# Scratch arrays of the last layer's weights laid out by chunks of 128 columns

## The chip, the core and the metric

One core of a Trainium2 chip runs the whole program. The metric is the device time of one execution in microseconds (us), taken as the median of several runs. The engines are PE (matrix products, TensorE), DVE (VectorE), ACT (ScalarE), POOL (GpSimd) and SP, which here only issues transfers. All transfers go through one queue, SP's, in program order.

## The reference

Windowed attention over 4 batches, 8 heads, 576 positions and head size 64 gives x with 2304 rows of 512 columns. Two feed-forward layers follow; the change is in what serves the second one's output product:

```python
gate = 1.0 / (1.0 + np.exp(-(x @ w_gate)))          # 512 -> 1536
x = gate * (x @ w_val) @ w_out                       # 1536 -> 512
h = x @ w_in                                         # 512 -> 2048
g = np.maximum(h, 0.0) + alpha * np.minimum(h, 0.0)
out = g @ moe2_w_out                                 # 2048 -> 512
```

## The kernel before, in words

Every large product is done in float16 with each factor split into a high and a low half, so three matmuls stand for one (high by high, high by low, low by high). The second layer's two products use a seven-product scheme over 2x2 blocks: seven combinations of the weight's blocks times seven combinations of the data's blocks. So the weight `moe2_w_out` (2048 by 512, called `w_out2`) is turned into seven float16 arrays of 1024 by 256, each as high and low half. That is done beside the matmuls of the first layer, in these steps:

- `out2_load`, `out2_decode`, `out2_bound`, `out2_store` (L763 to L784): for each chunk `c` of 128 columns (4) and each half `h` of the rows (2), the weight is read, decoded to float32 by DVE, and stored to the scratch array `plain_dram`.
- `out2_sum` and `out2_power` (L786, L790) make one scale for all of it, from the largest sums.
- For four pieces `(q, c)`, called here the first to the fourth: `out2_fetch` (L796) reads the four blocks of the piece back into two `quarter` tiles; `out2_sums` (L804) makes four combinations on POOL (L810 to L813); `out2_high` (L816) makes the high halves on ACT (L820); `out2_low` (L822) the low halves on DVE (L825); `out2_put` (L834) stores them to the scratch array `w2_dram` (L838). The seven products of a piece lie in four `halves` tiles: products 1 and 2, 3 and 5, 6 and 7, and 4 alone, called tiles A, B, C and D below.
- `w2_fetch` (L1189) later reads one whole product into SBUF, and `out2_mm` (L1195) uses it as the moving operand, 256 columns at a time (L1210).

The `quarter`, `halves`, `words`, `y` and `ys` tiles share one pool of eight buffers (`yp`). A new tile waits until what last used its buffer is done: a store that reads it, or an engine that does. ACT, DVE, POOL and SP each work strictly in program order, so one that waits holds back all that stands behind it. The program counts transfers on eight counters used in turn, so a transfer also waits until the one eight places ahead of it has landed.

The order is written out by hand: a queue of `steps`, each with a cost, is worked off by `prepare` between groups of matmuls. In the last batch (`late`), the output product of the first layer (`o1_mm`, L632) runs through four column groups d = 0 to 3 of 72 matmuls each. `last_output` puts the start of the second layer between them: `y_load` at the start of d = 0 and d = 1, `y_sums` (POOL, L901), `y_high` (ACT, L924) and `y_low` (DVE, L928) in d = 1, and the first matmuls of the second layer (`in2_mm`, L967) after the first 6 matmuls of d = 2. These need `yh`, which ACT and DVE make behind all of `out2_high` and `out2_low`.

Of the kernel before, what the change touches and what calls it, by code (L numbers as in the profile page):

```python
# [8 lines left out]
F32 = mybir.dt.float32  # L9
F16 = mybir.dt.float16  # L10
# [14 lines left out]
def attention_moe_kernel(  # L25
# [22 lines left out]
    nc = tc.nc  # L48
    P = 128
# [4 lines left out]
    NT, DM = out.shape  # L54
    F1 = w_out.shape[0]
    F2 = w_out2.shape[0]
    KD = DM // P
    M1 = F1 // P
    M2 = F2 // P
    U = M2 // 2  # L60
    H4 = DM // 2
# [8 lines left out]
    wp = ctx.enter_context(tc.tile_pool(name="wp", bufs=1))  # L70
# [3 lines left out]
    dp = ctx.enter_context(tc.tile_pool(name="dp", bufs=1, space=bass.MemoryType.DRAM))  # L74
# [410 lines left out]
    plain = {}  # L485
    wt = {}

    def stage():
        return wp.tile([P, 8, P], F32, tag="st", name="plain", bufs=2)

    def flat(t):

        return t.rearrange("p k f -> p (k f)")
# [187 lines left out]
    yh = {}  # L681
    w2p = None
    wi_dram = dp.tile([U, P, 2, 7, 2 * P], F16, name="wi_dram")
    plain_dram = dp.tile([P, M2, DM], F32, name="plain_dram")
    w2_dram = dp.tile([7, P, 2, U, H4], F16, name="w2_dram")

# [91 lines left out]

    def out2_store(c, h):
        nc.sync.dma_start(
            out=plain_dram[:, 8 * h:8 * h + 8, P * c:P * c + P], in_=plain.pop(("2", c, h))
        )  # L784

    def out2_sum():  # L786
# [9 lines left out]
    def out2_fetch(q, c):  # L796

        for h in range(2):
            t = quarter[h] = yp.tile([P, 2, 4, P], F32, tag="y", name="quarter")
            for i in range(2):  # L800
                f = H4 * i + P * c
                nc.sync.dma_start(out=t[:, i], in_=plain_dram[:, 8 * h + 4 * q:8 * h + 4 * q + 4, f:f + P])

    def out2_sums(q, c):  # L804

# [16 lines left out]
    def out2_low(q, c, which):  # L822
        for i in which:
            t = plain["h", q, c, i]
            nc.vector.scalar_tensor_tensor(  # L825
                out=t[:, 1], in0=plain["q", q, c][i], scalar=s_2, in1=t[:, 0], op0=ALU.mult, op1=ALU.subtract
            )
        for a in last_put:
            out2_put(*a)
        last_put[:] = [(q, c, which)]  # L830
# [3 lines left out]
    def out2_put(q, c, which):  # L834
        for i in which:
            t = plain.pop(("h", q, c, i))
            for z in range(2):
                nc.sync.dma_start(  # L838
                    out=w2_dram[i - 1, :, z, 4 * q:4 * q + 4, P * c:P * c + P],
                    in_=t[:, z].rearrange("p (k f) -> p k f", k=4),  # L840
                )

    def alpha_scale():

# [334 lines left out]
    ring = deque()  # L1179
    sums2 = {}  # L1180

    def w2_ring(first):
        if first:
            ring.append([flat(stage()).bitcast(F16).rearrange("p (k f) -> p k f", f=H4) for _ in range(2)])
        else:
            t = wp.tile([P, 3, 2, U, H4], F16, name="w_2", tag="w_o")
            ring.extend([t[:, i, z] for z in range(2)] for i in range(3))

    def w2_fetch(i):  # L1189
# [5 lines left out]
    def out2_mm(j, i, k):  # L1195
        n = blocks[j][1] // 2
        nt = n // P
        first = {1: True, 6: True, 5: True}.get(i, False)
        bank = "xyz"[{1: 0, 2: 0, 6: 1, 7: 1, 4: 1, 5: 2, 3: 2}[i]]
        if first and k == 0:  # L1200
            turn["o"] = (turn.get("o", -1) + 1) % 4
            sums2[bank] = banks[:, turn["o"], :]
        ps, w, g = sums2[bank], w2q[i][0], g2[j, i, k // 2]
        h = g[0][:, :, n * (k % 2):n * (k % 2) + n]
        for t in range(nt):
            c = slice(P * t, P * t + P)
            for z, (a, x_) in enumerate(
                ((h[:, 0, c], w[0][:, k, :]), (h[:, 0, c], w[1][:, k, :]), (h[:, 1, c], w[0][:, k, :]))
            ):
                nc.tensor.matmul(  # L1210
                    ps[:, H4 * t:H4 * t + H4], lhsT=a, rhs=x_, start=(first and k == 0 and t == 0 and z == 0),
                    stop=(k == U - 1 and z == 2), skip_group_check=True,
                )
        g[1] -= 1
        if not g[1]:
            h, _, home = g2.pop((j, i, k // 2))
            if home:
                home[1] -= 1
                h = home[0]
            if not home or not home[1]:  # L1220
                places2.append(h)
        if k == U - 1:
            ring.append(w2q[i].popleft())
            out2_done(j, i, ps[:, :H4 * nt], nt)

    def out2_done(j, i, ps, nt):
        n = H4 * nt
        s_ = total[:, j:j + 1]
        e, u2, u3 = (temps[x_][:, :n] for x_ in ("e", "u2", "u3"))
        dst = {1: e, 6: u2, 2: u3, 7: u3, 5: u3, 4: e, 3: u2}[i]  # L1230
        to = {2: (0, 0), 5: (1, 1), 4: (1, 0), 3: (0, 1)}.get(i)
        if i in (1, 2):
            nc.scalar.activation(dst, ps, AF.Copy, scale=s_)
        else:
            nc.vector.scalar_tensor_tensor(
                out=dst, in0=ps, scalar=s_, in1={6: e, 7: e, 5: u3, 4: e, 3: u2}[i], op0=ALU.mult, op1=ALU.add
            )
        if to:
            r0 = blocks[j][0] + P * nt * to[0]
            nc.sync.dma_start(  # L1240
                out=out[r0:r0 + P * nt, H4 * to[1]:H4 * to[1] + H4].rearrange("(t p) c -> p t c", p=P),
                in_=dst.rearrange("p (t c) -> p t c", c=H4),
            )
# [64 lines left out]
    with tc.manual_schedule():  # L1308
# [66 lines left out]
        for n in range(2 * KD):  # L1375
            c, h = n // 2, n % 2
            step(4, lambda c=c, h=h: out2_decode(c, h, 0))
            step(
                4, lambda c=c, h=h: out2_decode(c, h, 1),
                lambda n=n: out2_load((n + 1) // 2, (n + 1) % 2) if n + 1 < 2 * KD else None,  # L1380
                lambda n=n: out2_store((n - 1) // 2, (n - 1) % 2) if n else in2_store(U - 1),
            )
            step(0, lambda c=c, h=h: out2_bound(c, h), apart=1)
        order = [dict(q=q, c=c) for c in range(2) for q in range(2)]
        step(3, lambda: out2_store(KD - 1, 1), lambda: out2_fetch(**order[0]))
        step(1, out2_sum, out2_power, sums=True, apart=3)
        for n, a in enumerate(order):
            step(0, lambda a=a: out2_sums(**a), lambda n=n: out2_fetch(**order[n + 1]) if n < 3 else None)
            step(0, lambda a=a: out2_high(**a, which=(1, 2)))
            step(3, lambda a=a: out2_high(**a, which=(3, 5)), lambda a=a: out2_low(**a, which=(1, 2)))  # L1390
            step(3, lambda a=a: out2_high(**a, which=(6, 7)), lambda a=a: out2_low(**a, which=(3, 5)))
            step(3, lambda a=a: out2_high(**a, which=(4,)), lambda a=a: out2_low(**a, which=(6, 7)))
            step(2, lambda a=a: out2_low(**a, which=(4,)))
# [117 lines left out]
        i = 2 * turn["m"]  # L1511
# [169 lines left out]
```

## Time and profile before

| what | value |
|---|---|
| runs | 909.71, 910.52, 911.55 us; median 910.52 |
| profiled execution | 908.63 us; its span in the profile 906.8 us |
| mean granted clock of PE | 0.971 of full |
| PE, DVE, ACT, POOL busy | 843.8, 677.8, 450.8, 303.4 us |
| transfers | 166.81 MB in 120439 packets, mean 184 GB/s |

PE is busy 93% of the span, so the question is where its idle time lies and what ends it. In the profile's row of 40 slices, the 24th (521 to 544 us) is the one after the start-up in which PE's busy share falls, to 7 tenths, and its granted clock to 6 tenths; the transfer engines are at 9 tenths there.

### The profile page before, as it was taken

Reading aid. Unit: us, or ns where it says so; the run is one execution under the profiler, and the core shown is the slowest. Engines: PE = TensorE matmul, PEld = TensorE weight load, DVE = VectorE, ACT = ScalarE, POOL = GpSimd, SP = SyncE. Lnnn points to the kernel's source line nnn. Section 1 sums busy time; section 2 is a strip of 40 time slices with the busy share of each in tenths; the row PEclk is TensorE's granted clock in tenths of the full one; section 3 lists DMA queues with packets and bytes.
Section 4 is the critical chain, followed back from the end, with each engine's and each line's share of the span. In section 5 each row is a group of like instructions: output and inputs, shape, how many; then the busy total and the mean of one; then the engine's idle time right before and its main releaser. Section 6 shows DMA issues by size and latency. Waiting matters only on the chain.

```text
span 906.8 us, 19500 instructions
## 1 busy us (share of the span) xinstructions
PE 843.8 (93%) x8196; PEld 696.4 (77%) x8196; DVE 677.8 (75%) x1039; ACT 450.8 (50%) x739; POOL 303.4 (33%) x264
## 2 busy tenths in 40 slices
PE   7778778899999999999999959997999999999998
PEld 5566566687777877778788738886788888888887
DVE  6999999726978757767795647678888878886751
ACT  5676555444444445534435356555456456545430
POOL 2455656500202001111125643335344454243220
PEclk9899899799999999999999969998999999999999
DMA  9763435115215615009758995955765695575462
GB/s 325 263 227 129 146 117 170 40 46 178 81 51 180 199 49 200 25 2 306 247 157 224 242 256 195 338 218 184 267 263 187 214 343 187 197 258 208 143 215 85
DMA packets 120439, 166.81 MB, mean 184 GB/s; under 512 B 34464, under 2 KB 96032, under 8 KB 120352
## 3 DMA queue, kind: packets, MB, share of 16 engines
q1 hardware_dynamic: 120352, 165.58, 54.4%
q8 instruction: 64, 1.05, 0.5%
q14 instruction: 23, 0.19, 0.1%
HBM read 137.24 MB, written 28.31 MB: 183 GB/s over the span
## 4 chain that ended last, share of the span: by engine, by line
PE 59%; DVE 24%; ACT 6%; DMA 5%; issue 3%; SPq 2%; POOL 0%; ACTq 0%; POOLq 0%; DVEq 0%
PE banks L590 16%; PE banks L1210 14%; PE banks L967 13%; PE banks L632 12%; DVE plain L183 4%; DVE plain L187 3%; DVE plain L179 2%; PE banks L437 2%; DMA w_dram<-halves 2%; DVE temp_w L1013 2%; DVE temp_y L1013 1%; DVE gf L608 1%; DVE g_gv L1052 1%; PE banks L323 1%; DMA words<-w_gate 1%
## 5 line engine op out<-in xcount | busy, mean ns | idle before, releaser
L590 PE MATMUL banks<-xh,w_gv 128*128 128x288 f16 x2304 | 294.6, 289 | 1.5 <-ACT sg L603 1.5
L590 PEld LDWEIGHTS <-w_gv 128*128 128x128 f16 x2304 | 224.8, 99 | 60.8 <-issue 1.8
L967 PE MATMUL banks<-yh,w_i 128*128 128x256 f16 x1536 | 191.2, 276 | 19.2 <-ACT yh L924 9.9
L967 PEld LDWEIGHTS <-w_i 128*128 128x128 f16 x1536 | 151.6, 99 | 40.7 <-issue 20.4
L632 PE MATMUL banks<-gt,w_o 128*128 128x288 f16 x1152 | 148.8, 290 | 1.6 <-POOL gt L168 1.5
L632 PEld LDWEIGHTS <-w_o 128*128 128x128 f16 x1152 | 113.0, 99 | 32.2 <-issue 1.8
L1210 PEld LDWEIGHTS <-g_gv 128*128 128x128 f16 x780 | 76.6, 98 | 9.2
L1210 PE MATMUL banks<-w,g_gv 128*128 128x256 f16 x612 | 75.5, 273 | 0.0
L164 POOL TENSOR_SCALAR sc<-sc 128x1 f32<-128x1 f32 x35 | 12.5, 357 | 178.8 <-DVE sc L160 178.7
L1062 POOL TENSOR_TENSOR yh<-temp_y 128x512 f32<-128x512 f32 x16 | 27.1, 1692 | 131.5 <-DVE temp_y L1013 126.8
L194 ACT ACTIVATE junk<-plain 128x1024 bf16<-128x1024 f32 (+1 forms) x36 | 36.3, 1009 | 59.5 <-DVE plain L198 30.1
L187 DVE SCALAR_TENSOR_TENSOR plain<-words,plain 128x512 uint32<-128x512 uint32 x68 | 63.8, 959 | 1.2
L1013 DVE SCALAR_TENSOR_TENSOR temp_w<-neg,sc,temp_w 128x256 f32<-128x256 f32 x48 | 55.5, 1194 | 10.9 <-ACT neg L1005 10.8
L1210 PEld LDWEIGHTS <-g_g 128*128 128x128 f16 x564 | 55.2, 98 | 6.4
L183 DVE SCALAR_TENSOR_TENSOR plain<-words,plain 128x512 uint32<-128x512 uint32 x68 | 58.8, 885 | 1.2
L168 POOL TENSOR_TENSOR gt<-gf,gt 128x576 f16<-128x576 f32 x24 | 36.9, 1538 | 66.4 <-ACT gt L615 66.4
L608 DVE SCALAR_TENSOR_TENSOR gf<-banks,sg 128x576 f32<-128x576 f32 x48 | 36.0, 749 | 30.6 <-PE banks L590 30.1
L603 ACT ACTIVATE sg<-banks,sc 128x576 f32<-128x576 f32 x48 | 35.2, 734 | 34.3 <-PE banks L590 25.2
L615 ACT ACTIVATE gt<-gf 128x576 f16<-128x576 f32 x48 | 32.3, 676 | 39.0 <-DVE gf L608 39.0
L1210 PE MATMUL banks<-w,g_g 128*128 128x256 f16 x396 | 48.3, 273 | 0.0
L179 DVE TENSOR_SCALAR plain<-words 128x512 uint32<-128x512 uint32 x68 | 40.2, 611 | 7.8 <-DMA plain_dram<-plain 3.9
L388 POOL TENSOR_TENSOR s<-s,rs 128x1152 f32<-128x1152 f32 (+1 forms) x9 | 17.8, 1977 | 71.4 <-DVE rs L383 64.1
(170 smaller groups left out, 1284.1 us busy)
## 6 DMA issues: line engine op xcount, KB each, us to landing
w_i<-wi_dram SPq DMA_DIRECT2D x40, 896.0 KB, 6.3
w<-w_dram SPq DMA_DIRECT2D x52, 512.0 KB, 8.5
words<-w_out SPq DMA_DIRECT2D x28, 512.0 KB, 5.4
plain<-w_dram SPq DMA_DIRECT2D x18, 512.0 KB, 8.5
words<-w_in SPq DMA_DIRECT2D x16, 512.0 KB, 5.1
w_dram<-halves SPq DMA_DIRECT2D x56, 128.0 KB, 2.6
q<-qbd SPq DMA_DIRECT2D x6, 1152.0 KB, 6.5
words<-w_gate SPq DMA_DIRECT2D x12, 512.0 KB, 5.1
```

What stands on the lines that cost most here:

```text
L168: engine.tensor_tensor(out=lo, in0=src, in1=hi, op=ALU.subtract)
L179: nc.vector.tensor_scalar(out=d, in0=hi, scalar1=3, scalar2=0x3FFFFFFF, op0=ALU.logical_shift_left, op1=ALU.bitwise_and)
L183: nc.vector.scalar_tensor_tensor(out=d, in0=hi, scalar=0xC0000000, in1=d, op0=ALU.bitwise_and, op1=ALU.bitwise_or)
L187: nc.vector.scalar_tensor_tensor(out=d, in0=lo, scalar=29, in1=d, op0=ALU.logical_shift_right, op1=ALU.bitwise_or)
L194: nc.scalar.activation(junk[:, :src.shape[1]], src, AF.Square, accum_out=dst)
L590: nc.tensor.matmul(ps[:, h, :], lhsT=a, rhs=x_[:, H2 * h:H2 * h + H2], start=(kk == 0 and i == 0), stop=(kk == KD - 1 and i == 2),)
L603: nc.scalar.activation(halves(sg), ps, AF.Sigmoid, scale=sgx[b][:, m:m + 1])
L608: nc.vector.scalar_tensor_tensor(out=halves(gf), in0=ps, scalar=2.0 ** -15, in1=halves(sg), op0=ALU.mult, op1=ALU.mult)
L632: nc.tensor.matmul(ps[:, h, :], lhsT=a, rhs=x_[:, H2 * h:H2 * h + H2], start=(m == 0 and z == 0), stop=(m == M1 - 1 and z == 2),)
L967: nc.tensor.matmul(o, lhsT=h, rhs=l, start=(new and v == 0 and q == 1), stop=(q == total_), skip_group_check=True,)
L1013: nc.vector.scalar_tensor_tensor(out=temps[x_][:, c], in0=t[:, c], scalar=slope[:, u + v:u + v + 1], in1=src[:, c], op0=ALU.mult, op1=ALU.add,
L1210: nc.tensor.matmul(ps[:, H4 * t:H4 * t + H4], lhsT=a, rhs=x_, start=(first and k == 0 and t == 0 and z == 0), stop=(k == U - 1 and z == 2) ...
```

## The change

The two scratch arrays get another layout, so that what one transfer moves for one partition lies in a row in DRAM. A store of `plain_dram` moves 4 KB in a row for each partition (before, 8 rows of 512 bytes), a load of a quarter 2 KB (before, 4 rows of 512 bytes), a store of `w2_dram` 1 KB for each half (before, 4 rows of 256 bytes), with both halves in one transfer. A load of a whole product from `w2_dram` stays at 4 KB in a row. In SBUF its columns now lie as two chunks, so the matmul's moving operand is two rows of 128 columns, 2 KB apart, where it was one row of 256.

```diff
-    plain_dram = dp.tile([P, M2, DM], F32, name="plain_dram")
-    w2_dram = dp.tile([7, P, 2, U, H4], F16, name="w2_dram")
+    plain_dram = dp.tile([P, KD, M2, P], F32, name="plain_dram")
+    w2_dram = dp.tile([7, P, 2, 2, U, P], F16, name="w2_dram")
     def out2_store(c, h):
-            out=plain_dram[:, 8 * h:8 * h + 8, P * c:P * c + P], in_=plain.pop(("2", c, h))
+            out=plain_dram[:, c, 8 * h:8 * h + 8], in_=plain.pop(("2", c, h))
     def out2_fetch(q, c):
-                f = H4 * i + P * c
-                nc.sync.dma_start(out=t[:, i], in_=plain_dram[:, 8 * h + 4 * q:8 * h + 4 * q + 4, f:f + P])
+                nc.sync.dma_start(out=t[:, i], in_=plain_dram[:, 2 * i + c, 8 * h + 4 * q:8 * h + 4 * q + 4])
     def out2_put(q, c, which):
-            for z in range(2):
-                nc.sync.dma_start(
-                    out=w2_dram[i - 1, :, z, 4 * q:4 * q + 4, P * c:P * c + P],
-                    in_=t[:, z].rearrange("p (k f) -> p k f", k=4),
-                )
+            nc.sync.dma_start(
+                out=w2_dram[i - 1][:, :, c, 4 * q:4 * q + 4].rearrange("p z k f -> p z (k f)"), in_=t
+            )
     def w2_ring(first):
-            ring.append([flat(stage()).bitcast(F16).rearrange("p (k f) -> p k f", f=H4) for _ in range(2)])
+            ring.append([flat(stage()).bitcast(F16).rearrange("p (c k f) -> p c k f", c=2, k=U) for _ in range(2)])
-            t = wp.tile([P, 3, 2, U, H4], F16, name="w_2", tag="w_o")
+            t = wp.tile([P, 3, 2, 2, U, P], F16, name="w_2", tag="w_o")
     def out2_mm(j, i, k):
-                ((h[:, 0, c], w[0][:, k, :]), (h[:, 0, c], w[1][:, k, :]), (h[:, 1, c], w[0][:, k, :]))
+                ((h[:, 0, c], w[0][:, :, k, :]), (h[:, 0, c], w[1][:, :, k, :]), (h[:, 1, c], w[0][:, :, k, :]))
-                    ps[:, H4 * t:H4 * t + H4], lhsT=a, rhs=x_, ...
+                    ps[:, H4 * t:H4 * t + H4].rearrange("p (c f) -> p c f", c=2), lhsT=a, rhs=x_, ...
```

The order on PE, ACT, DVE and POOL stays; only line numbers behind L834 fall by 2 or 3. On SP, the rows from the fetch of the fourth piece to the last store, before:

```order
L802 DMA quarter<-plain_dram 128x4x128 x4
L838 DMA w_dram<-halves 128x4x128 x2
L757 DMA w_i_5829<-wi_dram 128x3584
L869 DMA y<-y_dram 128x2x256 x2
L838 DMA w_dram<-halves 128x4x128 x18
L652 DMA y_dram<-y 128x576
L869 DMA y<-y_dram 128x2x512 x2
L838 DMA w_dram<-halves 128x4x128 x10
```

The same rows of the changed kernel:

```order
L801 DMA quarter<-plain_dram 128x512 x4
L836 DMA w_dram<-halves 256x1x512
L757 DMA w_i_5829<-wi_dram 128x3584
L866 DMA y<-y_dram 128x2x256 x2
L836 DMA w_dram<-halves 256x1x512 x9
L652 DMA y_dram<-y 128x576
L866 DMA y<-y_dram 128x2x512 x2
L836 DMA w_dram<-halves 256x1x512 x5
```

The stores are half as many (28 where there were 56 in all), and nothing has changed places.

On ACT, what the high halves of the third and the fourth piece wait for, before. `DMAHW0` to `DMAHW7` are the eight counters of transfers; four of them together are the four stores of the tile that had the buffer before, two of them the two stores of a tile D.

```order
L820 ACTIVATE halves_6257<-quarter_6096,sc_78 128x512 [waits DMAHW2_49,DMAHW7_49,DMAHW1_49,DMAHW0_49]
L820 ACTIVATE halves_6286<-quarter_6099,sc_78 128x512 [waits DMAHW5_49,DMAHW4_49,DMAHW6_49,DMAHW3_49,Activation_49]
L820 ACTIVATE halves_6314<-plain_6245,sc_78 128x512 [waits DMAHW0_49,DMAHW7_49,Activation_49,Pool_49]
L820 ACTIVATE halves_6323<-plain_6246,sc_78 128x512 [waits DVE_49,Pool_49]
L820 ACTIVATE halves_6366<-quarter_6251,sc_78 128x512 [waits DMAHW6_49,DMAHW5_49,DMAHW7_49,DMAHW4_49,DMAHW3_49]
L820 ACTIVATE halves_6369<-quarter_6254,sc_78 128x512 [waits DMAHW2_49,DMAHW3_49,DMAHW1_49,DMAHW0_49]
L820 ACTIVATE halves_6400<-plain_6360,sc_78 128x512 [waits DVE_49,Pool_49]
L820 ACTIVATE halves_6448<-plain_6361,sc_78 128x512 [waits DMAHW1_49,DMAHW0_49]
```

And of the changed kernel, for the same eight instructions (tiles A, B, C and D of the third piece, then of the fourth):

```order
L819 ACTIVATE halves_6244<-quarter_6090,sc_78 128x512 [waits DMAHW2_49,DVE_49]
L819 ACTIVATE halves_6273<-quarter_6093,sc_78 128x512 [waits DMAHW5_49,DMAHW3_49,DMAHW2_49]
L819 ACTIVATE halves_6300<-plain_6232,sc_78 128x512 [waits DVE_49,Pool_49]
L819 ACTIVATE halves_6307<-plain_6233,sc_78 128x512 [waits DVE_49]
L819 ACTIVATE halves_6346<-quarter_6238,sc_78 128x512 [waits DMAHW7_49,DMAHW6_49]
L819 ACTIVATE halves_6349<-quarter_6241,sc_78 128x512 [waits DMAHW1_49,DMAHW0_49]
L819 ACTIVATE halves_6379<-plain_6340,sc_78 128x512 [waits DVE_49,Pool_49]
L819 ACTIVATE halves_6425<-plain_6341,sc_78 128x512 [waits DVE_49]
```

The pool hands out other buffers: of the eight first writes six waited for stores before, and three do now (tile B of the third piece, on the two stores of the second piece's tile B; tiles A and B of the fourth, on the two stores of the third's tiles A and B). Tile A of the third piece now waits for its own quarter load and for DVE's low half of the second piece's product 7; tile C for POOL's last sum of the third piece; tile D for DVE.

## Rows read from the trace of the kernel before

**Rows 1.** Page, part 4: the chain that ended last, share of the span by engine.

```profile
PE 59%; DVE 24%; ACT 6%; DMA 5%; issue 3%; SPq 2%; POOL 0%; ACTq 0%; POOLq 0%; DVEq 0%
```

**Rows 2.** Windows: stretch, length, PE PEld DVE ACT POOL busy, PE clock, DMA share, GB/s.

```profile
507.00:518.00 11.00, 9.51 (x78) 7.35 (x76) 6.32 (x7) 3.55 (x6) 8.89 (x7) 1.00 0.92 215
...
528.00:537.00 9.00, 0.37 (x1) 0.10 (x1) 5.33 (x8) 6.63 (x11) 1.30 (x2) 0.61 1.06 227
537.00:545.00 8.00, 6.06 (x33) 4.07 (x33) 2.28 (x5) 3.52 (x7) 5.62 (x8) 0.59 1.07 270
```

**Rows 3.** Timeline of PE, 505 to 546: start, length, what, [idle before <- releaser].

```profile
517.61 10.21 PE L632 MATMUL banks<-gt,w_o 128*128 128x288 f16 x82 [1.49 <-POOL gt L168]
536.54 0.37 PE L967 MATMUL banks<-yh,w_i 128*128 128x256 f16 x1 [8.72 <-ACT yh L924]
537.38 0.58 PE L967 MATMUL banks<-yh,w_i 128*128 128x256 f16 x2 [0.46 <-DVE yh L928]
539.11 0.37 PE L967 MATMUL banks<-yh,w_i 128*128 128x256 f16 x1 [1.15 <-ACT yh L924]
539.89 4.13 PE L967 MATMUL banks<-yh,w_i 128*128 128x256 f16 x20 [0.41 <-DVE yh L928]
```

**Rows 4.** Waits of ACT, 485 to 546: total, times, longest.

```profile
ACT halves L820 <- DMA w_dram<-halves: 16.0, 5, 6.2
```

**Rows 5.** Timeline of ACT, 505 to 540.

```profile
511.98 1.33 ACT L820 ACTIVATE halves<-quarter,sc 128x512 f16<-128x512 f32 x2 [4.68 <-DMA w_dram<-halves]
...
515.00 0.67 ACT L615 ACTIVATE gt<-gf 128x576 f16<-128x576 f32 x1
521.89 0.72 ACT L820 ACTIVATE halves<-plain,sc 128x512 f16<-128x512 f32 x1 [6.22 <-DMA w_dram<-halves]
...
528.97 1.33 ACT L820 ACTIVATE halves<-quarter,sc 128x512 f16<-128x512 f32 x2 [4.10 <-DMA w_dram<-halves]
...
532.50 0.72 ACT L820 ACTIVATE halves<-plain,sc 128x512 f16<-128x512 f32 x1 [0.27 <-DVE halves L825]
...
535.78 0.71 ACT L924 ACTIVATE yh<-y,sc 128x512 f16<-128x512 f32 x1
```

**Rows 6.** Timelines of DVE and POOL, same stretch.

```profile
503.53 1.76 DVE L825 SCALAR_TENSOR_TENSOR halves<-plain,sc,halves 128x512 f16<-128x512 f32 x1
...
506.54 0.74 DVE L825 SCALAR_TENSOR_TENSOR halves<-quarter,sc,halves 128x512 f16<-128x512 f32 x1
...
512.62 1.27 POOL L813 TENSOR_TENSOR plain<-quarter,plain 128x512 f32<-128x512 f32 x1
515.74 1.82 POOL L168 TENSOR_TENSOR gt<-gf,gt 128x576 f16<-128x576 f32 x1 [1.85 <-ACT gt L615]
...
523.53 1.65 POOL L810 TENSOR_TENSOR plain<-quarter 128x512 f32<-128x512 f32 x1 [5.71 <-DVE halves L825]
...
528.04 1.26 POOL L813 TENSOR_TENSOR plain<-quarter,plain 128x512 f32<-128x512 f32 x1
```

**Rows 7.** SP: issue times of L838 (ns, min/median/max), us to landing.

```profile
L838 SPq DMA_DIRECT2D w_dram<-halves x56: 359/488/3152, 488.4 to 544.1; - x56
...
DMA to landing us min/median/max: 2.0/2.6/7.6
```

**Rows 8.** Transfers in 489:497 (stores alone), 700:860 (large ones), 476:545: packets, MB, share.

```profile
q1 hardware_dynamic: 5011, 1.30, 76.8%
...
q1 hardware_dynamic: 9904, 34.87, 59.4%
...
q1 hardware_dynamic: 39872, 16.48, 95.3%
```

**Rows 9.** Matmuls by line (ns, min/median/max), and the chain's last stretch: start, length.

```profile
L309 PE MATMUL banks<-mask_sb x12: 322/326/481, 4.5 to 133.3; 128*128 128x384 bf16 x12
...
L1210 PE MATMUL banks<-w,g_gv x252: 272/273/273, 716.7 to 859.3; 128*128 128x256 f16 x126
...
864.86 38.00 PE banks L1210 x348
```

More of the change, by code (lines that the diff above doesn't have):

```diff
@@ L1207, in out2_mm @@
             for z, (a, x_) in enumerate(
-                ((h[:, 0, c], w[0][:, k, :]), (h[:, 0, c], w[1][:, k, :]), (h[:, 1, c], w[0][:, k, :]))
+                ((h[:, 0, c], w[0][:, :, k, :]), (h[:, 0, c], w[1][:, :, k, :]), (h[:, 1, c], w[0][:, :, k, :]))
             ):
                 nc.tensor.matmul(
-                    ps[:, H4 * t:H4 * t + H4], lhsT=a, rhs=x_, start=(first and k == 0 and t == 0 and z == 0),
+                    ps[:, H4 * t:H4 * t + H4].rearrange("p (c f) -> p c f", c=2), lhsT=a, rhs=x_, start=(first and k == 0 and t == 0 and z == 0),
                     stop=(k == U - 1 and z == 2), skip_group_check=True,
```

## The prediction

> **What bounds the kernel now.** I read the chain of waits by engine first. Most of it is PE, and a transfer ends only 5% of it, issuing on SP 2% [rows 1]; so the whole is no transfer-bound kernel, and the question is where that 5% lies. The table by windows answers it: PE is busy 9.51 of 11 us from 507, 0.37 of 9 from 528 and 6.06 of 8 from 537, and the transfer engines stand at 0.92 to 1.07 there [rows 2]. PE's own timeline splits this into a wait of 1.49 us for POOL's `gt` and four waits for `yh`, 8.72, 0.46, 1.15 and 0.41 us, in all 12.23 us [rows 3]. After the long one the granted clock is 0.61 and 0.59, that is partly at the lower level of 1.2 GHz [rows 2], and the 20 matmuls from 539.89 take 4.13 us, 206 ns each [rows 3]; at full clock one takes 38.00 / 348 = 109 ns [rows 9].
>
> Who is late for `yh`? ACT makes it, at 535.78, behind all the high halves of the weight. ACT's waits in this stretch are led by stores of `halves`: 16.0 us in 5 waits [rows 4], 4.68 us before the third piece, 6.22 us before its tile C, 4.10 us before the fourth piece [rows 5]. The buffers are all in use, and they come free only when 256-byte stores have landed. So here PE waits for ACT, ACT for buffers, and buffers for stores.
>
> **The change part by part.** *Transfer time.* Between 489 and 497 us nearly only stores of `halves` ran: 0.768 x 8 us x 16 engines / 5011 packets = 19.6 ns each, of 1.30 MB / 5011 = 259 bytes. Between 700 and 860 us large ones ran: 0.594 x 160 x 16 / 9904 = 153.5 ns each, of 3521 bytes [rows 8]. A line through both is 9.0 ns and 0.041 ns a byte: an estimate of 30 ns for 512 bytes, 51 for 1 KB, 93 for 2 KB, 177 for 4 KB. The 56 stores of 128 KB are 28672 packets, 35.1 us of 16 engines; as 7168 packets of 1 KB, 22.8. The 16 quarter loads of 256 KB go from 15.4 to 11.9 us, the 8 stores of `plain` from 15.4 to 11.3. So 15.8 us go out of the 0.953 x 69 = 65.8 us that 476 to 545 holds (a part of the stores lands later). The stores of `plain` come earlier, while PE does not stop; I count them at nothing.
>
> The rows give 13.2 GB/s for one engine at 259 bytes and 22.9 at 3521 [rows 8], and none at 512 alone. The Trainium skill (DMA: Bandwidth & Descriptors, Specifications) has 512 bytes as the least size for full rate, with read-modify-write below it. By that rule the quarter loads, at 512 bytes already, would gain nothing, and 12.3 us would go rather than 15.8: the engines would be busy for 53.5 of 69 us rather than 50.0, which speaks for the first rival below.
>
> *Issuing.* A store takes SP 0.49 us in the middle, 3.15 at most [rows 7]. 28 fewer save 13.7 us of SP, all in this stretch. On the other side a store now waits for DVE's low half, where the high half's own store could go ahead; behind it on SP stand the next stores, the fetch of the next piece, `w_i` and the loads of `y`. That is one DVE instruction more, 0.74 us, or 1.76 beside POOL [rows 6], for a tile whose buffer needed both halves stored anyway.
>
> *Waits of ACT.* Here the order decides. Tile A of the third piece waits now for DVE's low half of the second piece's product 7, which ends at 506.54 + 0.74 = 507.28 [rows 6], so it starts at 507.3 where it was 511.98: 4.6 us earlier. Tile B waits for the stores of the second piece's tile B. DVE has those halves at 503.53 + 1.76 = 505.29 [rows 6]; with 0.5 us to issue and 2.6 us to land, the middle value [rows 7], that is 508.4, when ACT, two instructions of 0.67 us behind 507.3, comes to it anyway. Then `gt` follows some 3.0 us behind tile A, as now (515.00 - 511.98) or a little more, at 510.9 [rows 5]. POOL can take it when L813 ends, 512.62 + 1.27 = 513.89 [rows 6], and with 1.3 to 1.8 us has it at 515.7. PE wants it at 517.61 - 1.49 = 516.12 [rows 3]: the first wait is gone by a narrow margin.
>
> Tile C waited for stores till 521.89; it now waits for POOL's L813, 513.89. ACT's two instructions and DVE's low half put the low half of product 6 at about 516.4, and that is what POOL's L810 of the fourth piece waits for. Its four sums took 528.04 + 1.26 - 523.53 = 5.77 us [rows 6]: 522.2 where it was 529.3.
>
> The fourth piece's tiles A and B wait for the stores of the third's A and B. SP comes to these behind the last store of the second piece's tile C (507.28 + 0.5), four loads of the fourth piece (2 us, at 0.5 each like a store), the store of the second piece's tile D (out at 510.3), one `w_i` and two loads of `y`, the second of which takes the buffer of that tile D: 510.3 + 2.6, so 513 to 514 with 0.5 us for itself. The two stores of A are out at 514.5 and land at 517 to 518.5. I take 518.5 for tile A, where it was 528.97, and 520 for tile B; ACT is then held by POOL's sums until 522.2 to 522.8, so 1.5 us more or less here changes nothing. From there to the first `yh` it took 535.78 - 532.50 = 3.28 us [rows 5]; with 0.4 us for DVE's last halves, 526.5 where it was 535.78.
>
> *PE.* Without the wait of 1.49 us, PE is through with d = 1 at 517.61 + 10.21 - 1.49 = 526.3 [rows 3]. It meets the first `yh` at 527.2. The tail from ACT's first `yh` to continuous matmuls was 539.89 - 535.78 = 4.1 us, of it 1.45 us waiting for POOL's `ys`, whose buffer comes free earlier now; I take 2.8 us, so 529.3. Hence 539.89 - 529.3 = 10.6 us. With a stop of about 2.3 us in bits the clock should stay: the wait of 1.49 us left it at 1.00, the one of 8.72 us did not [rows 2, 3]. Then the 20 matmuls take 2.2 us rather than 4.13, another 1.9 us. After that nothing in the chain to the end hangs on these transfers, and all is shifted as it is.
>
> *The matmul's two rows.* In the trace no matmul reads two rows at a distance. The nearest is L309, which reads the same 64 columns six times: 326 ns for 384 columns, against 273 for 256 in one row [rows 9]. The difference, 53 ns, is 128 columns at 2.4 GHz: five row ends cost nothing that shows. The bound above is that a row start costs what a matmul has over its columns: 109.2 - 256 / 2.4 GHz = 2.5 ns, and 1512 matmuls (7 products, 8 blocks of rows, three terms, 9 groups of 256 tokens) would make 3.8 us. Below, a gain: nothing shortens a read, so 0. I take 0, since L309 is nearer.
>
> The Trainium skill (TensorE: Matmul & The Clock Gate, Wait — 56ns, not 53.3ns?) gives the same 2.5 ns as a cost of each matmul and not of a row. By it the term is 0, by the bound 3.8 us; no row settles it.
>
> **The sum.** 908.63 (the profiled execution: span 906.8 and 1.83 around it) - 10.6 - 1.9 = 896.1 us. The profiled execution lies 1.89 us under the median of the runs shown, so against that the forecast is 898.0 us.
>
> The ends of it: ACT cannot be faster than POOL's chain, which lets `yh` begin at 525.6 and PE run at 528.3; with `ys` in time that is 13.5 us in all, 897.0 by the median, and with DVE and POOL less in each other's way perhaps 2 us more, 895. Stores that still take 7.6 us to land, the longest seen [rows 7], put the second `y_load` at 517.9, the two stores behind it at 518.9 and tile A of the fourth piece at 526.5, only 2.5 us earlier than now: 908.0.
>
> **The rivals.** *The wait comes back elsewhere (0.20).* Tiles A and B of the fourth piece still wait for stores, through SP's order and its wait for DVE. If stores take 4 to 6 us to land rather than 2.6, twice in a row (for the second load of `y`, then for tile A), that is 3 to 7 us later, of which 1.5 is slack, and a stop of that length brings the lower clock back, 1.9 us: 5 to 9 us are left, 901.5 to 905.5. For it: the engines stay busy for 50.0 of 69 us, 0.72. Against: the waits of ACT fall from six to three by the order itself, and the median landing is 2.6 us.
>
> *No change (0.05).* POOL and DVE set the pace of the four pieces rather than the stores, and PE's wait is only renamed: 910.5. Against: around tile C of the third piece ACT is idle for 6.22 us for stores and POOL for 5.71 us behind it [rows 5, 6], so neither sets the pace there.
>
> *Slower by the matmul (0.07).* Each of the 1512 output matmuls pays for its second row, on PE, in a stretch where PE is the chain without a gap to the end [rows 9]. At 2.5 ns it costs 3.8 us, and 901.8 comes out, still faster. It decides from 12.5 / 1512 = 8.3 ns; at 10 ns, 15.1 us, the time is 913.1. For it: nothing in the trace excludes it. Against: L309. A small cost of that kind, up to 8 ns, has 0.10 with times of 900 to 910, and is in the range.
>
> *It does not do what it says (0.02):* stores might still go out in 256-byte pieces; but in the changed program's rows a store is 256 rows of 512 elements, and in any case half of the issues are saved: 905.
>
> **How the numbers follow.** The forecast has 0.56, with 895 to 900; the wait coming back 0.20; a small row cost 0.10; the others 0.14. To leave out no more than 2 in 10 the range goes from 894.5 to 905.0. A measurement of this kernel can tell 0.2%, 1.8 us, from no change. Slower by that: 0.07, and 0.01 from the case without change. Same: 0.05, most of that case and a little of the row cost. Faster: 0.87.
>
> **What would show it.** Stores of `halves` x28 with 256 KB each, and packets under 512 bytes in 476 to 545 nearly gone. ACT's waits for stores under 5 us in all. `gt` of L168 no longer ending a wait of PE. PE's first matmul of the second layer (L964 in the changed kernel) before 529, its first run of 20 at 109 ns each, and a granted clock of 1.00 in the windows of 8 us around it. L1207 at 273 ns a matmul, 38.0 us for 348 at the end; 276 ns or 39 us would show the row cost. The forecast is wrong if ACT still waits over 10 us for stores, or if PE waits as long for another engine: for POOL's sums of the fourth piece, or for `ys`.

## Result and the profile after

| | before | after |
|---|---|---|
| median of the runs | 910.40 us | 900.96 us (900.78 to 902.26) |
| profiled execution, its span | 908.63, 906.8 us | 900.97, 899.2 us |
| mean granted clock of PE | 0.971 | 0.967 |
| PE, DVE, ACT, POOL busy | 843.8, 677.8, 450.8, 303.4 us | 850.2, 681.9, 450.4, 304.6 us |
| packets of all transfers | 120439 | 85176 |

The ratio is 0.9902 (95% interval 0.9889 to 0.9915): 9.4 us faster between the medians, where 12.5 were forecast. The mean clock and PE's busy time differ by how the first 200 us went, which changes from trace to trace with either layout: the granted clock of the first three times 50 us is 0.90, 0.97, 0.93 before, 0.83, 0.90, 0.86 after, and 0.90, 0.97, 0.93 again in kernel 6 below, which has the new layouts. So I count the stretch from its first high half (ACT's first `out2_high`). It comes 1.56 us later in the changed kernel (489.21, before 487.65), and "corrected" below means less 1.56. Line numbers behind L800 are 1 to 3 lower than before.

PE's timeline of the changed kernel (start, length, what, idle before and releaser):

```profile
518.42 10.21 PE L632 MATMUL banks<-gt,w_o 128*128 128x288 f16 x82 [0.89 <-POOL gt L168]
530.76 0.27 PE L964 MATMUL banks<-yh,w_i 128*128 128x256 f16 x1 [2.13 <-ACT yh L921]
531.60 0.49 PE L964 MATMUL banks<-yh,w_i 128*128 128x256 f16 x3 [0.57 <-DVE yh L925]
532.65 3.71 PE L964 MATMUL banks<-yh,w_i 128*128 128x256 f16 x20 [0.57 <-DVE yh L925]
```

The waits of [rows 3] are 12.23 us in sum; these are 4.16. But the 20 matmuls still take 3.71 us, 186 ns each, against 109 at full clock [rows 9]: the clock fell again. The windows show where (stretch, length, PE, PEld, DVE, ACT, POOL busy, granted clock, DMA share, GB/s):

```profile
507.00:518.00 11.00, 10.53 (x86) 8.27 (x85) 10.76 (x10) 5.83 (x9) 9.61 (x6) 1.00 1.02 362
528.00:537.00 9.00, 5.73 (x37) 4.05 (x35) 4.39 (x7) 6.20 (x13) 5.25 (x7) 0.81 0.82 256
537.00:545.00 8.00, 8.00 (x72) 6.88 (x71) 3.77 (x8) 3.17 (x8) 4.51 (x7) 1.00 0.69 247
```

Against [rows 2], PE is busy for 8 of the last 8 us where it was for 6.06, and from 507 to 518 the transfer engines move 362 GB/s where they moved 215. (In the page's row of 40 slices the 24th, named ahead of the prediction with 7 tenths for PE, stands at 5.) What changed on ACT is seen in its waits from 485 to 546 (total, times, longest) and in its timeline:

```profile
ACT halves L819 <- DMA w_dram<-halves: 6.1, 3, 2.6
...
ACT halves L819 <- POOL plain L812: 2.0, 1, 2.0
```

```profile
508.87 1.33 ACT L819 ACTIVATE halves<-quarter,sc 128x512 f16<-128x512 f32 x2
512.85 0.72 ACT L819 ACTIVATE halves<-quarter,sc 128x512 f16<-128x512 f32 x1 [2.65 <-DMA w_dram<-halves]
...
522.68 1.33 ACT L819 ACTIVATE halves<-quarter,sc 128x512 f16<-128x512 f32 x2 [2.34 <-DMA w_dram<-halves]
525.11 0.72 ACT L819 ACTIVATE halves<-quarter,sc 128x512 f16<-128x512 f32 x1 [1.09 <-DMA w_dram<-halves]
...
530.00 0.70 ACT L921 ACTIVATE yh<-y,sc 128x512 f16<-128x512 f32 x1
```

Of 16.0 us of waits for stores [rows 4] 6.1 are left, at the three places that the order left: tile B of the third piece, A and B of the fourth. What these wait for is in the stores' own rows (issue time in ns, min/median/max; us to landing):

```profile
L836 SPq DMA_DIRECT2D w_dram<-halves x28: 513/525/1307, 491.1 to 533.8; - x28
...
DMA to landing us min/median/max: 2.4/4.9/8.4
```

The middle one is 4.9 us, where it was 2.6 for half the size [rows 7]. But what counts is when those stores land that something waits for. The same rows for the second store of the second piece's tile B, the store of its tile D, and the two of the third piece's tile A:

```profile
L836 SPq DMA_DIRECT2D w_dram<-halves x1: 513/513/513, 506.9 to 506.9; - x1
...
DMA to landing us min/median/max: 5.9/5.9/5.9
...
L836 SPq DMA_DIRECT2D w_dram<-halves x1: 525/525/525, 512.4 to 512.4; - x1
...
DMA to landing us min/median/max: 5.0/5.0/5.0
...
L836 SPq DMA_DIRECT2D w_dram<-halves x2: 562/568/573, 518.1 to 518.8; - x2
...
DMA to landing us min/median/max: 3.8/3.8/3.8
```

506.9 + 5.9 = 512.8 is when ACT comes to tile B of the third piece (512.85). 512.4 + 5.0 = 517.4 is when SP can issue the second load of `y` (517.48), which needs tile D's buffer and has the stores of the third piece's tile A behind it. 518.8 + 3.8 = 522.6 is when ACT comes to tile A of the fourth piece (522.68).

The transfers of 491 to 499, stores with nothing else in the queue, and of 476 to 545 (packets, MB, share of 16 engines); last, of the kernel before, 478 to 482, where little but 512-byte rows of `plain_dram` moves:

```profile
q1 hardware_dynamic: 1094, 1.05, 38.5%
...
w_dram<-halves SPq DMA_DIRECT2D x6, 256.0 KB, 2.4
...
q1 hardware_dynamic: 12070, 18.28, 78.1%
...
q1 hardware_dynamic: 2139, 1.07, 100.1%
```

A store that has the queue to itself lands in 2.4 us in the middle; so I put the other 2.5 us of the median down to other transfers ahead of it and beside it, and kernel 8 below bears this out. A packet of 960 bytes took 0.385 x 8 x 16 / 1094 = 45.0 ns; the line of the prediction says 9.0 + 0.041 x 960 = 48. One of 500 bytes took 1.001 x 4 x 16 / 2139 = 29.9 ns; the line says 30 for 512. In 476 to 545 the engines were busy 53.9 us of 69, forecast 50.0; the window now also holds 1.80 MB more than [rows 8], which is another 4.9 us at 153.5 ns for 3521 bytes.

### The profile page after: what moved, and what is told of

Read it like the earlier page. It is cut to its first block, busy times and chain, and to the rows that moved or that the text cites. A ratio compares the mean times of both kernels' runs of the same rounds, so it can differ in the third digit from the quotient of the medians.

```text
span 899.2 us, 19438 instructions
## 1 busy us (share of the span) xinstructions
PE 850.2 (95%) x8196; PEld 701.5 (78%) x8196; DVE 681.9 (76%) x1039; ACT 450.4 (50%) x739; POOL 304.6 (34%) x264
## 2 busy tenths in 40 slices
DMA packets 85176, 166.81 MB, mean 186 GB/s; under 512 B 5345, under 2 KB 57697, under 8 KB 85089
## 4 chain that ended last, share of the span: by engine, by line
PE 57%; DVE 26%; ACT 6%; issue 4%; DMA 4%; POOL 1%; SPq 1%; ACTq 0%; DVEq 0%; POOLq 0%
PE banks L590 14%; PE banks L1207 14%; PE banks L964 13%; PE banks L632 12%; DVE plain L183 4%; DVE plain L187 3%; PE banks L437 3%; DVE plain L179 2%; DVE temp_w L1010 2%; DVE temp_y L1010 1%; DVE gf L608 1%; DVE halves L824 1%; DMA words<-w_gate 1%; DVE g_gv L1049 1%; PE banks L323 1%
## 5 line engine op out<-in xcount | busy, mean ns | idle before, releaser
L590 PE MATMUL banks<-xh,w_gv 128*128 128x288 f16 x2304 | 297.7, 291 | 1.5 <-ACT sg L603 1.5
```

What stands on the lines that cost most here:

```text
L590: nc.tensor.matmul(ps[:, h, :], lhsT=a, rhs=x_[:, H2 * h:H2 * h + H2], start=(kk == 0 and i == 0), stop=(kk == KD - 1 and i == 2),)
```

## The experiments

Ratios stand against runs of the kernel before on the same chip, with 95% intervals; 0.001 is 0.9 us. "From the first high half" is the span of the one profiled execution less the start of the stretch: 419.15 us before, 409.99 after, whatever the start-up did.

| kernel | ratio | interval | from first high half, us |
|---|---|---|---|
| changed kernel | 0.9902 | 0.9889 to 0.9915 | 409.99 |
| 1 only plain_dram new | 0.9985 | 0.9971 to 0.9999 | 416.3 |
| 2 only w2_dram new | 0.9918 | 0.9901 to 0.9935 | 412.1 |
| 3 two stores a product, 1 KB rows | 0.9936 | 0.9920 to 0.9953 | 412.8 |
| 4 one store a product, 256-byte pieces | 1.0005 | 0.9993 to 1.0016 | 419.3 |
| 5 one-row matmul | 0.9912 | 0.9898 to 0.9927 | 409.8 |
| 6 changed + own buffers | 0.9895 | 0.9880 to 0.9909 | 409.1 |
| 7 before + own buffers | 0.9921 | 0.9906 to 0.9936 | 412.2 |
| 8 changed + earlier w_i | 0.9915 | 0.9901 to 0.9928 | 411.6 |
| 9 own buffers + sums on DVE | 0.9816 | 0.9802 to 0.9829 | 403.8 |
| 10 own buffers + later places | 0.9846 | 0.9833 to 0.9859 | 406.1 |
| 11 changed + later places | 0.9889 | 0.9872 to 0.9906 | 408.4 |
| 12 changed + sums on DVE | 0.9885 | 0.9864 to 0.9905 | 409.7 |

**1 and 2: which array.** The diff of the change, cut in two: `plain_dram` with its stores and loads alone, then `w2_dram` with its puts, ring and matmul alone.

> Only the layout of plain_dram is new (stores 4 KB, quarter loads 2 KB in a row); w2_dram, its 56 stores of 256-byte pieces and the one-row matmul are the old ones. Theory (ACT's eight buffers are held by the stores of halves, and what counts is how soon those land): little, since the stores stay as they are; 3.5 us of transfer time go, and ACT's waits for stores stay at 12 to 16 us: 907 to 910 us, where 910.4 is the kernel before and 901.0 the changed one. Rival (the whole transfer time of the stretch counts, whoever's it is): 7.6 of the 15.8 us of transfer time went with this part, so about half of the 9.4 us, 905 to 906 us.

> Only the layout of w2_dram is new (28 merged stores with 1 KB rows, two-row matmul); plain_dram is the old one, its quarter loads in 512-byte rows. Theory (stores of halves hold the buffers): nearly the whole gain, 901 to 903 us, ACT's waits for stores at 6 to 8 us. Rival (all transfer time of the stretch counts): about half, 905 us.

908.63 us (0.9985) and 902.07 us (0.9918). As the theory had it, the weight's stores carry 7.5 us and the other array 1.4, together the whole; the smaller part is at the edge of its interval. In kernel 1 ACT waits 13.2 us for stores, in kernel 2 7.5.

**3 and 4: length of rows, or number of issues.** Kernel 3 is the changed one, kernel 4 the one before, each with the other's split:

```diff
 # 3
+            for z in range(2):
+                nc.sync.dma_start(out=w2_dram[i - 1][:, z, c, 4 * q:4 * q + 4].rearrange("p k f -> p (k f)"), in_=t[:, z])
 # 4
+            nc.sync.dma_start(out=w2_dram[i - 1, :, :, 4 * q:4 * q + 4, P * c:P * c + P],
+                              in_=t.rearrange("p z (k f) -> p z k f", k=4))
```

> The changed kernel with each product stored by two transfers again, one for the high and one for the low half: 56 stores of 128 KB with 1 KB rows. It has the new length of rows with the old number of issues and the old split of the waits. Theory A (the length of the rows makes the gain): 901 to 903 us; a store of 128 KB lands sooner than one of 256 KB (median under 4 us), and the high half need not wait for the low one. Theory B (half as many issues on SP make it, 13.7 us of SP): at most 3 us are left of the 9.4, 907 us or more.

> The kernel before with both halves of a product in one transfer: 28 stores of 256 KB, still in pieces of 256 bytes, one-row matmul, old plain_dram. Theory A (the length of the rows makes the gain): 907 to 911 us, ACT's waits for stores at 12 us or more, since 28672 packets at 19.6 ns still have to go. Theory B (the number of issues): 901 to 904 us.

903.65 us (0.9936) and 910.58 us (1.0005): kernel 3 a little above the range of its theory A, kernel 4 within it. Length without merging gives 5.8 us; merging without length nothing; merging on top of length 3 more. Kernel 3's stores, ACT's waits for them, and the longest of these waits:

```profile
L837 SPq DMA_DIRECT2D w_dram<-halves x56: 319/394/879, 489.6 to 538.5; - x56
...
DMA to landing us min/median/max: 1.9/2.6/7.2
```

```profile
ACT halves L819 <- DMA w_dram<-halves: 10.6, 3, 5.2
```

```profile
518.91 0.72 ACT L819 ACTIVATE halves<-plain,sc 128x512 f16<-128x512 f32 x1 [5.18 <-DMA w_dram<-halves]
```

Half of the stores of 128 KB land within 2.6 us, as theory A said, and yet ACT waits longer, 10.6 us against 6.1. The stores that it waits for are not the quick ones: the five issued from 517 to 519.5, the third piece's first, took 6.0 to 6.6 us. And the longest wait stands before tile C of the third piece, which in the changed kernel waits for POOL (2.0 us). So with the stores split the pool hands out other buffers, and counted from the first high half this tile starts 2.5 us later. So the last 3 us belong to merging together with the order of buffers that comes with it; the runs don't part the two.

Kernel 4 does not test the number of issues alone either. It has half of them, but a merged store of 256-byte pieces takes SP 0.83 us in the middle, so 28 x 0.83 = 23.2 us are left of 56 x 0.488 = 27.3. ACT waits 18.8 us for stores there. A median landing time alone doesn't price a wait; the place in SP's row belongs to it.

**5: the matmul's two rows.** The moving operand is read as `w[:, k // 4, 2 * (k % 4):2 * (k % 4) + 2, :]`, one row of 256.

> The changed kernel with the moving operand of the second layer's output product read as one row of 256 columns where the data lie as two chunks; this leaves the columns in the wrong order, so that part of the computation is changed, and its time is all that is read. Theory (two rows cost nothing): 901 us as the changed kernel, 273 ns a matmul. Rival (a second row costs up to 2.5 ns a matmul): up to 3.8 us less, 897 us, and 270 ns a matmul.

901.40 us (0.9912). The changed kernel's matmuls, then those of this kernel (by line; in the second, busy us and mean ns stand last):

```profile
L1207 PE MATMUL banks<-w,g_gv x612: 272/273/273, 584.8 to 892.4; 128*128 128x256 f16 x153
```

```profile
L1210 PE MATMUL banks<-w,g_gv 128*128 128x256 f16 x612 | 75.5, 273 | 0.0
```

Two rows cost nothing: 273 ns with either. That rules out the rival by the matmul, and the bound of 3.8 us.

**6 and 7: own buffers.** The third and fourth piece's tiles of `halves` get buffers where the first layer's weights lay, on the changed kernel and on the one before:

```diff
+    def own_tile(q, c, which):
+        if q not in own:
+            own[q] = wp.tile([P, 4, 2, 2, 4 * P], F16, name="own_halves", tag=f"w_gv{q}")
+        return own[q][:, (1, 3, 6, 4).index(which[0])]
     def out2_high(q, c, which):
-        t = yp.tile([P, 2, 2, 4 * P], F16, tag="y", name="halves")
+        t = own_tile(q, c, which) if c else yp.tile([P, 2, 2, 4 * P], F16, tag="y", name="halves")
```

> The changed kernel with the third and fourth piece's tiles of halves in buffers of their own (16 KB a partition each, in the pool of the first layer's weights, free by then), so that no high half waits for a store. Theory (the shortfall of 3 us against the forecast is the 6.1 us that ACT still waits for stores, and the clock that falls behind the stop): ACT waits only for loads and POOL, the stop of PE shrinks from 4.2 to under 2.5 us, 20 matmuls in 2.2 us: 896 to 898.5 us. Rival (POOL's sums and ys set the pace now): 900 to 901 us, with PE's stop ended by POOL's ys or the load of y, which stand in SP's queue behind the same stores.

> The kernel before, with its two old layouts, and the same own buffers for the third and fourth piece's tiles of halves. Theory (stores matter only through the buffers they hold): nearly all of what the changed kernel gains, or more, without any change of layout, 898 to 902 us. Rival (the transfer time itself is in the way: loads of quarters and of y are late behind 256-byte stores): 904 to 909 us, with ACT or POOL waiting for loads in place of stores.

899.72 us (0.9895) and 902.22 us (0.9921). Own buffers alone give the old kernel 7.2 us with all its 256-byte stores. PE's waits for `yh` fall from 10.74 us to 2.52, against 2.44 in kernel 6, and PE is continuous 42.53 us after the first high half, against 42.45. So what these stores cost in this stretch, they cost through the buffers they hold; the 2.4 us that ACT now waits for loads of quarters, as the rival said, hardly reach PE. The rest shows later: with the old layouts PE waits five times for loads of `w_i`, 4.0 us in all, where kernel 6 has one such wait of 1.0 (PE's timeline of kernel 7, 550 to 580):

```profile
552.54 1.48 PE L974 MATMUL banks<-yh,w_i 128*128 128x256 f16 x12 [0.58 <-DMA w_i<-wi_dram]
554.73 1.48 PE L974 MATMUL banks<-yh,w_i 128*128 128x256 f16 x12 [0.70 <-DMA w_i<-wi_dram]
574.27 0.83 PE L974 MATMUL banks<-yh,w_i 128*128 128x256 f16 x6 [0.65 <-DMA w_i<-wi_dram]
576.45 3.78 PE L974 MATMUL banks<-yh,w_i 128*128 128x256 f16 x33 [1.34 <-DMA w_i<-wi_dram]
```

But on the changed kernel the same buffers gain hardly anything: the intervals overlap, and from the first high half it is 0.9 us. My theory, that the waits for stores are the whole shortfall, fell here. No high half waits for a store any more, and PE still stops (kernel 6, PE's timeline, DVE's timeline, and the window from 517):

```profile
529.15 0.49 PE L971 MATMUL banks<-yh,w_i 128*128 128x256 f16 x3 [1.87 <-DVE yh L932]
530.21 3.97 PE L971 MATMUL banks<-yh,w_i 128*128 128x256 f16 x20 [0.57 <-DVE yh L932]
```

```profile
519.74 5.10 DVE L831 SCALAR_TENSOR_TENSOR own_halves<-quarter,sc,own_halves 128x512 f16<-128x512 f32 x3
524.76 2.35 DVE L831 SCALAR_TENSOR_TENSOR own_halves<-plain,sc,own_halves 128x512 f16<-128x512 f32 x2
527.04 0.74 DVE L831 SCALAR_TENSOR_TENSOR own_halves<-quarter,sc,own_halves 128x512 f16<-128x512 f32 x1
```

```profile
517.00:528.00 11.00, 10.29 (x83) 8.09 (x83) 11.00 (x10) 7.59 (x14) 9.49 (x7) 1.00 0.99 326
```

DVE is busy 11.00 of 11 us. Its low halves take 5.10 / 3 = 1.70 us each while POOL makes its sums, and 0.74 once POOL is through. So a second chain, DVE held up by POOL, ends nearly when the stores did, and takes their place. The Trainium skill (SBUF — State Buffer, SBUF: two separate sides) says that a DVE operation with two SBUF inputs and a POOL operation that reads SBUF exclude each other at a shared pair of ports for a whole instruction. The durations agree in that both engines slow down beside each other (POOL's sums from 1.27 to some 1.7 us); but one of each, 0.74 + 1.27 = 2.01 us, would take longer in turn than the 1.70 measured, so the trace does not show that they exclude each other for the whole of an instruction.

**8: fetches of w_i earlier.** `if late and m in (3, 4, 5, 6):` in place of `(5, 7, 9, 11)`.

> The changed kernel with the four last fetches of w_i (each 0.9 MB) behind groups 3 to 6 of their batch in place of 5, 7, 9 and 11, so that they are out of the way of the stores of the third piece. Theory (the stores land late, 4.9 us in the middle, because loads of quarters and of w_i are ahead of them in the one queue): landing nearer to 2.6 us, ACT's waits for stores under 4 us, 898 to 900 us. Rival (stores of 256 KB take that long by themselves, or the fetches only move the crowd to the first two pieces): 901 us or more.

901.54 us (0.9915). The stores landed sooner, 3.5 us in the middle, and ACT's waits for them fell to 2.1 us by this view, as expected; the time did not follow. ACT waited for POOL instead:

```profile
ACT halves L819 <- POOL plain L812: 3.7, 1, 3.7
...
ACT halves L819 <- DMA w_dram<-halves: 2.1, 2, 1.5
```

Another 1.6 us, before tile B of the fourth piece, which ACT starts at 523.69, stand in the trace without a releaser; the second store of the third piece's tile B was issued at 518.5 and landed 5.1 us later, so that is a wait for a store too. The first `yh` comes 40.67 us after the first high half, where it came after 40.79: the rival, 901 us or more, held.

**9 and 12: POOL's sums on DVE**, with own buffers and without. One word of `out2_sums` is changed:

```diff
-        add = nc.gpsimd.tensor_tensor
+        add = nc.vector.tensor_tensor
```

> The kernel with own buffers, and the four sums of each piece (128x512, float32) made by DVE in place of POOL. In the kernel with own buffers no high half waits for a store, DVE is busy for 11.0 of the 11 us from 517 to 528, and a low half takes DVE 1.70 us there, beside POOL's sums, where it takes 0.74 us alone. Theory (what is left of the stop is DVE, held up by POOL): low halves at 0.75 us, sums under 1 us each, so 7 x 0.75 + 4 x 0.8 = 8.5 us a piece where DVE took some 10, the last low half 2 us earlier, the stop of PE ended by ys or the load of y or gone: 896.5 to 899 us. Rival (DVE's length of work rules, not who is beside it): 16 sums more on DVE make it 8 us later or more, the stop of PE grows to over 6 us, 903 us or more.

> The changed kernel with the four sums of each piece on DVE in place of POOL, and no own buffers: one word is changed. With both, PE did not stop at all and the time was 893.8 us, 0.9816 of before. Theory (DVE beside POOL was what was left of the stop, stores a small part; their wait is filled by other work of ACT and DVE): a stop of at most 1.5 us, the clock at 1.00, 894 to 896.5 us, 0.982 to 0.985. Rival (pieces that come faster only wait longer for the stores, which still take 4.9 us to land): ACT's waits for stores rise from 6 us to 10 us or more, 898 to 901 us, 0.986 to 0.990.

893.84 us (0.9816) and 899.62 us (0.9885). Kernel 9 on DVE, 518 to 527, and its windows:

```profile
518.06 0.68 DVE L809 TENSOR_TENSOR plain<-quarter 128x512 f32<-128x512 f32 x1
...
520.58 2.54 DVE L831 SCALAR_TENSOR_TENSOR own_halves<-quarter,sc,own_halves 128x512 f16<-128x512 f32 x3
523.05 1.88 DVE L831 SCALAR_TENSOR_TENSOR own_halves<-plain,sc,own_halves 128x512 f16<-128x512 f32 x2
524.85 0.74 DVE L831 SCALAR_TENSOR_TENSOR own_halves<-quarter,sc,own_halves 128x512 f16<-128x512 f32 x1
```

```profile
519.00:528.00 9.00, 9.00 (x76) 7.20 (x74) 9.00 (x14) 6.34 (x12) 2.33 (x2) 1.00 1.07 371
528.00:537.00 9.00, 9.00 (x81) 7.68 (x80) 1.85 (x5) 2.62 (x6) 5.59 (x8) 1.00 0.87 303
```

A sum takes 0.68 us on DVE where it took POOL some 1.7, and a low half 0.94 or less on the mean of each of these rows. PE has no gap and the clock stays at 1.00. DVE does 16 instructions more and, counted from the first high half, is through with the low halves 4.3 us sooner than in kernel 6. The time is 2.7 us below the range of the theory. Without own buffers the same word gives next to nothing: the pieces come faster and wait longer for stores, 9.5 us, as the rival said (kernel 12, ACT's waits, then PE's timeline):

```profile
ACT halves L819 <- DMA w_dram<-halves: 9.5, 3, 3.6
```

```profile
528.53 0.27 PE L964 MATMUL banks<-yh,w_i 128*128 128x256 f16 x1 [1.98 <-ACT yh L921]
529.37 0.49 PE L964 MATMUL banks<-yh,w_i 128*128 128x256 f16 x3 [0.57 <-DVE yh L925]
530.90 4.01 PE L964 MATMUL banks<-yh,w_i 128*128 128x256 f16 x20 [1.04 <-DVE yh L925]
```

So the two chains lie side by side: take one away and 0.3 to 0.9 us are gained from the first high half (12, 6), take both and 6.2 (9). Of these 6.2, PE's waits in the changed kernel, 4.16 us, and the slow 20 matmuls, 3.71 - 20 x 0.109 = 1.5 us, make 5.7.

**10 and 11: later places of the second layer's first parts**, with own buffers and without:

```diff
-            if d > 1 and M1 * (d - 2) + m in (1, 4, 6, 9, 11, 14, 16, 19):
+            if d > 1 and M1 * (d - 2) + m in (5, 8, 10, 12, 14, 16, 18, 20):
```

> The kernel with own buffers, and the eight first parts of the second layer stand four to six groups of six matmuls later among the groups of d = 2 and d = 3, so that 24 matmuls more of the first layer (3.3 us) lie between the end of d = 1 and the first one that needs yh. Theory (the rest of the stop and the lower clock behind it, some 1.6 us, are what is left): no wait for yh, granted clock 1.00, 2 to 4.5 us less than the kernel with own buffers (899.7 us): 895 to 898 us. Rival (the work is only moved, and PE waits later for the results of the parts that come late): within 1 us of 899.7, with new waits for ACT's or DVE's results between 545 and 620.

> The changed kernel with the same later places of the second layer's first parts and no other change. Theory: most of its stop of 4.2 us is covered by 3.3 us of matmuls, the clock stays at 1.00: 896.5 to 899 us. Rival (only moved): 900 to 902 us.

896.64 us (0.9846) and 900.78 us (0.9889). With own buffers 24 matmuls more cover the stop and the clock stays up: 4.5 us by the ratios, 3.0 from the first high half. On the changed kernel the stop is covered too (PE's timeline of kernel 11):

```profile
518.80 13.15 PE L632 MATMUL banks<-gt,w_o 128*128 128x288 f16 x106 [0.88 <-POOL gt L168]
531.78 0.78 PE L964 MATMUL banks<-yh,w_i 128*128 128x256 f16 x4
533.13 2.34 PE L964 MATMUL banks<-yh,w_i 128*128 128x256 f16 x20 [0.57 <-DVE yh L925]
```

The 20 matmuls take 2.34 us. But new waits for loads of `w_i` follow at 559.84 and 562.02 (1.71 and 0.70 us), and the interval overlaps that of the changed kernel: theory and rival each have a part, and the ratio cannot settle how large.

## Why the prediction was right, and where 3 us went

The forecast case said 895 to 900 by the median; 900.96 lies a little above it, and short of 901.5 to 905.5, the times of the rival "the wait comes back elsewhere". The mechanism forecast is the one that made the gain (kernels 1, 2, 7). But the rival's condition came true as well: two landings in a row of 4 to 6 us, or nearly (5.0 us ahead of the second load of `y`, then 3.8 and 4.9 for tiles A and B of the third piece), and the lower clock behind the stop. It cost less than the rival had it: tile A of the fourth piece came 2.6 us late, not 3 to 7. So the time fell between the two cases, and that it lies in the range is partly luck: the range was drawn over both but for the rival's last half us.

- **Tile A of the third piece:** forecast 507.3, measured 508.87, corrected 507.3. The wait of 4.68 us [rows 5] is gone.
- **Stores land in 2.6 us: the mis-sized term.** They took 4.9 in the middle, and 5.9, 5.0, 3.8 and 4.9 where something waited for them. Tile B of the third piece, forecast free of waiting at 508.65, started at a corrected 511.3. Tile A of the fourth: 521.1 for 518.5, most of it because tile D's store landed at a corrected 515.9 where 510.3 + 2.6 = 512.9 was forecast; tile B 523.55 for 520. The 2.6 was the median of stores half as large, and I knew the merged ones would stand behind loads of quarters and of `w_i`; a store alone in the queue already takes 2.4.
- **`gt`:** PE's wait did not go, it fell from 1.49 to 0.89 us. It is POOL's, not the stores': 0.88 also in kernel 6, and gone in kernel 9. I had given POOL's sums the durations that they have without DVE beside them, up to 513.89; DVE, freed of waiting, was now beside them, and the last sum ended at a corrected 515.13.
- **First `yh`:** 528.44 for 526.5. **PE continuous:** a corrected 531.1 for 529.3: 8.8 us instead of 10.6. Kernel 6 splits the 1.8 us that are missing. From the first high half PE is continuous after 41.65 us by the forecast, 43.44 in the changed kernel and 42.45 with own buffers: 1.0 us goes with the stores' waits, and 0.8 stays, which kernel 9 shows to be DVE beside POOL. The two chains overlap, so the split holds for taking the stores' waits away first.
- **The clock stays at 1.00: wrong, 1.5 us.** Forecast 1.9 us, got 4.13 - 3.71 = 0.42. I took a stop "in bits" to be like the wait of 1.49 us. It isn't: in kernel 6 a stop of 2.44 us, with three matmuls recorded between its two parts, was enough. The granted clock was 0.72 in the 6 us behind it, and the 20 matmuls took 3.97 us. The loss does not follow the length of the stop (3.71 us after 3.27 in the changed kernel), and why stays open. Where PE had worked up to some 1.2 us before them (kernel 11), they took 2.34.
- **Two rows cost nothing:** right (kernel 5). **Transfer time:** right within what the rows can tell. The line through packet sizes gave 48 ns where 45.0 were measured, and 30 where 29.9 were. One engine moved 16.7 GB/s with 500-byte packets, 21.3 with 960-byte ones and 22.9 with 3521-byte ones. The Trainium skill (DMA: Bandwidth & Descriptors, Specifications) has 512 bytes as the least size for full rate; here longer packets still gain, so that rule, which I weighed, does not fit this queue.
- **SP's 13.7 us of issues** I had listed without a price of their own, and the runs give them none: kernel 4, which gained nothing, saved only 4.1 us of them, and the 3 us of kernel 3 come with another order of buffers.

The sum closes on the profiled executions: 908.63 - 8.8 - 0.42 + 1.56 = 900.97 us, as measured.

**What beats both kernels:** kernel 9, 893.84 us, 0.9816 (0.9802 to 0.9829) of before. A later place was not tried on top of it; PE has no stop there to cover. Nor was kernel 9 run with the old layouts, so what the change of layout still adds beside own buffers and sums on DVE is not shown.

## What to carry to other kernels

When a transfer is slow because of small pieces, look for what waits on it: here a pool of buffers, and buffers of their own gave most of the gain without touching a layout. Before sizing such a gain, ask which chain ends second, and price its instructions with the neighbours they will then have, not with those of the trace: two chains that end together hide each other's gain until both are shortened. And a landing time is that of a transfer at its place in the queue; take it from transfers that stand behind the same neighbours, and from those that something waits for, not from the median of all.

## What the runs showed that I had not expected

- A low half on DVE takes 0.74 us alone and 1.70 beside POOL's sums; moving 16 sums of 1.7 us from POOL to DVE, at 0.68 each, shortened DVE's own chain, and with free buffers the kernel by 7 us (0.9895 to 0.9816; 5.4 us from the first high half).
- The merged store's time to land: 2.4 us alone in the queue, 4.9 in the middle of the mixture, 8.4 at most.
- PE's clock fell after a stop of 2.4 us broken by three recorded matmuls, and cost 1.6 us behind it (3.97 against 2.34 for 20 matmuls), two thirds of the stop itself.
